# Seven half-block products for eight in the second mixture of an attention-and-two-mixtures kernel

## The chip, the cores and the metric

The kernel runs on one core of a Trainium2 chip. The metric is device time in microseconds (us), from the start of the program to its end; less is better. A core has a matrix engine (TensorE, PE in the profile; its weight loads are PEld), a vector engine (VectorE, DVE), an activation engine (ScalarE, ACT), GpSimd (POOL) and a queue that starts transfers (SyncE, SP). Products are collected in eight banks of PSUM, which DVE and ACT empty.

## The reference, cut to what matters

```
x  = attention(q, k, v)               # 4 batches, 8 heads, 576 positions, 64 wide -> 2304 tokens x 512
a, b = x @ w1, x @ w2                 # first mixture: 512 -> 1024
y  = ((a * b) @ w3) @ w_out           # 2304 x 512
h  = max(y @ v1, y @ v2, y @ v3)      # second mixture: 512 -> 768
out = h @ v_out                       # 768 -> 512
```

All data are float32 on both sides, and the weights reach the chip as 64-bit words from which the kernel makes 32-bit numbers.

## The kernel before, in words

The kernel has two halves. Attention and the first mixture are woven together, then comes the second mixture ("B" in the code), which is what the change rewrites.

Tokens lie along the free axis, in chunks of N = 512 columns (four of 512, one of 256). A number is kept as two parts, a high part that the matrix engine takes whole and the rest (`split`, L351: the high part on ACT at L352, the low part on DVE at L354). One product of a 128x128 weight block with a chunk is therefore three matmuls (`mm3`, L358 to L361).

For each chunk and each f of the hidden width, `front` (L648) makes the products with w1 and w2 (first mixture) or v1, v2, v3 (second), 12 matmuls each. The first product is copied out of PSUM by ACT (L663), the others are multiplied in, or joined by maximum, by DVE (L665). The result is split into g. `back` (L670) multiplies g by the output weights into four banks that stay open over all f; it runs one f behind. `finish_a` (L692) writes y to DRAM, `load_y` (L725) reads it back in the order of the output, and `finish_b` (L713) copies the last result out and stores it.

Weights of the second mixture are made at the end of the first: `pair` (L385) loads two 512 KB blocks of words into the place of weights that are no longer used, turns them into float32 (`float32`, L372: one ACT and four DVE instructions), and splits them. They then stay in SBUF for all chunks.

The order of all instructions is worked out ahead by a planner (`Program`, L111): each task has an engine and an estimated cost, PE tasks marked `chained` keep the order of the program, everything else is placed by how late it may be. `order` (L150) tries 30 plans, the later ones with random shifts, and keeps the one with the earliest modelled end. So any change of the tasks draws a new plan for the whole kernel, attention included. A tile that reuses a slot waits for the slot's last tile to be finished. All transfers but those of L410 are issued by SP, in order.

Of the kernel before, what the change touches and what calls it, by code (L numbers as in the profile page):

```python
# [61 lines left out]
N = 512  # L62
# [7 lines left out]
LAG = 1  # L70
MM = 0.175
# [13 lines left out]

class Tile:


    def __init__(self, slot, shape, dtype, name, ap=None):
        self.among = slot if isinstance(slot, list) else None  # L90
        self.slot = None if self.among else slot
        self.shape, self.dtype, self.name, self.ap = shape, dtype, name, ap
        self.before = self.slot.last.tasks if self.slot and self.slot.last else []
        if self.slot:
            self.slot.last = self
        self.tasks, self.touched, self.left = [], [], None

    def __call__(self):
        if self.ap is None:
# [8 lines left out]
class Program:  # L108
# [8 lines left out]
    def add(self, options, fn, reads=(), writes=(), chained=False, size=0):  # L117
# [14 lines left out]
        for what, writing in ((reads, False), (writes, True)):  # L132
            for x in what:
# [6 lines left out]
                x.tasks.append(t.n)  # L140
        deps.discard(t.n)
# [8 lines left out]
    def order(self, rounds=30):  # L150
# [8 lines left out]
        best, shift, tries = None, {}, Random(0)  # L159
# [131 lines left out]
def attention_moe_kernel(ctx, tc, q0, k0, v0, mask0, ql, kl, vl, mask, qkp, vp, w12, w3t, wo, m123, mo, out):  # L291
# [19 lines left out]
    xr, gr, cvr, zr, er, orr = ring("x", 2), ring("g", 2), ring("cv", 2), ring("z", 2), ring("e", 1), ring("o", 2)  # L311
    tqr, kr, qr, vwr, vdr = ring("tq", 2), ring("k", 4), ring("q", 4), ring("vw", 2), ring("vd", 3)
# [4 lines left out]
    others = banks[4:]  # L317

# [39 lines left out]
    def mm3(o, whi, wlo, xhi, xlo, first, last):  # L358
        nc.tensor.matmul(o, wlo, xhi, start=first, stop=False)  # L359
        nc.tensor.matmul(o, whi, xlo, start=False, stop=False)  # L360
        nc.tensor.matmul(o, whi, xhi, start=False, stop=last)  # L361
# [142 lines left out]
    def slab(n):  # L504
# [64 lines left out]
        for h2 in range(HP // 2):  # L569
# [23 lines left out]
            for ch, c0, c1 in spans(n):  # L593
                c, w = n * SL + c0 - ch * N, c1 - c0
                part = lambda i, h2=h2, xt=xs["A", ch], c=c, w=w: xt()[:, i, h2 * 2:h2 * 2 + 2, c:c + w]
                split(lambda part=part: part(0), lambda part=part: part(1),
                      lambda x32=x32, c0=c0, c1=c1: x32()[:, :, c0:c1], 2 * w, [x32], xs["A", ch])
# [4 lines left out]
    def weights_product():  # L602
# [21 lines left out]
        for half in range(2):  # L624
            prog.group += 1
            os = [Tile(b, [P, 512], F32, "pw") for b in acc]
# [21 lines left out]
    def front(kind, ch, f):  # L648
        prog.group += 1
        xt, n = xs[kind, ch], WIDTHS[ch]  # L650
        ws = [wa[f, i] if kind == "A" else wb[f, i] for i in range(2 if kind == "A" else 3)]
        z, pps = zr.tile([P, N], F32, "z"), []
        for i, (dw, w) in enumerate(ws):
            pp = bank("pf")

            def products(e, w=w, pp=pp):
                for k in range(KX):
                    c = slice(k * P, (k + 1) * P)
                    mm3(pp()[:, :n], w()[:, 0, c], w()[:, 1, c], xt()[:, 0, k, :n], xt()[:, 1, k, :n], k == 0, k == KX - 1)

            prog.add(mm(n, 12), products, [dw, xt], [pp], chained=True)
            if i == 0:
                prog.add(act(n), lambda e, pp=pp: e.copy(z()[:, :n], pp()[:, :n]), [pp], [z])  # L663
            else:
                prog.add(psum(n), lambda e, pp=pp: e.tensor_tensor(  # L665
                    z()[:, :n], pp()[:, :n], z()[:, :n], op=ALU.mult if kind == "A" else ALU.max), [pp], [z])
        g = gs[kind, ch, f] = gr.tile([P, 2, N], F32R, "g")
        split(lambda: g()[:, 0, :n], lambda: g()[:, 1, :n], lambda: z()[:, :n], n, [z], g)

    def back(kind, ch, f):  # L670
        prog.group += 1
        g, n = gs[kind, ch, f], WIDTHS[ch]
        dw, w = wa[f, 2] if kind == "A" else wb[f, 3]
        last = (NF if kind == "A" else NF2) - 1
        if f == 0:
            accs[0] = [Tile(b, [P, N], F32, "py") for b in acc]
        os = accs[0]
        for l in range(KX):

            def products(e, l=l):  # L680
                c = slice(l * P, (l + 1) * P)
                mm3(os[l]()[:, :n], w()[:, 0, c], w()[:, 1, c], g()[:, 0, :n], g()[:, 1, :n], f == 0, f == last)

            prog.add(mm(n, 3), products, [dw, g], [os[l]], chained=True)
        if f == last:
            for l in range(KX):
                (finish_a if kind == "A" else finish_b)(ch, l, os[l])

    y_dram = [[Tile(None, None, F32, "y", dram.tile([P, NB2, S], F32, name=f"y_dram{r}_{l}")) for l in range(KX)]
              for r in range(NR)]  # L690

    def finish_a(ch, l, src):  # L692
        o, n = orr.tile([P, N], F32, "o"), WIDTHS[ch]
# [200 lines left out]
```

## Time and profile before

| | us |
|---|---|
| median of 3 runs | 801.55 (801.49 to 803.25) |
| the profiled execution | 803.03 |
| its span, first to last instruction | 801.0 |
| PE busy in the span | 761.4 |
| DVE busy | 373.9 |
| ACT busy | 299.9 |

The profiled execution took 2.03 us more than its span. Matmuls overlap, so the duration of one (about 0.39 us for 512 columns) is longer than the spacing at which they follow each other; spacing is what counts for a stream of them. "Granted clock" is the share of full TensorE speed that the chip allowed in a stretch (1.00 is 2.4 GHz, 0.50 is 1.2 GHz).

### The profile page before, as it was taken

Reading aid. Unit: us, or ns where it says so; the run is one execution under the profiler, and the core shown is the slowest. Engines: PE = TensorE matmul, PEld = TensorE weight load, DVE = VectorE, ACT = ScalarE, POOL = GpSimd, SP = SyncE. Lnnn points to the kernel's source line nnn. Section 1 sums busy time; section 2 is a strip of 40 time slices with the busy share of each in tenths; the row PEclk is TensorE's granted clock in tenths of the full one; section 3 lists DMA queues with packets and bytes.
Section 4 is the critical chain, followed back from the end, with each engine's and each line's share of the span. In section 5 each row is a group of like instructions: output and inputs, shape, how many; then the busy total and the mean of one; then the engine's idle time right before and its main releaser. Section 6 shows DMA issues by size and latency. Waiting matters only on the chain.

```text
span 801.0 us, 15559 instructions
## 1 busy us (share of the span) xinstructions
PE 761.4 (95%) x6512; PEld 597.7 (75%) x6512; DVE 373.9 (47%) x672; ACT 299.9 (37%) x691; POOL 52.1 (7%) x130
## 2 busy tenths in 40 slices
PE   2989769999999989999999999999999999999997
PEld 0434458777777778777888899888888888888897
DVE  5899978456322543244421469995211322211211
ACT  3475746455425542454211346542201401121021
POOL 1220320022000210010000000000000000000000
PEclk9989859999999999999999999999999999999999
DMA  9897631033311322111330098401100100010010
GB/s 342 232 364 256 168 75 51 31 94 54 95 38 49 84 55 68 51 24 29 95 102 0 4 316 312 138 1 52 60 1 0 54 1 0 1 53 0 1 53 28
DMA packets 52390, 68.78 MB, mean 86 GB/s; under 512 B 23712, under 2 KB 39072, under 8 KB 52320
## 3 DMA queue, kind: packets, MB, share of 16 engines
q1 hardware_dynamic: 47712, 64.25, 24.6%
q0 software_dynamic: 4608, 3.55, 3.2%
q8 instruction: 51, 0.84, 0.5%
q14 instruction: 19, 0.16, 0.1%
HBM read 58.33 MB, written 9.44 MB: 85 GB/s over the span
## 4 chain that ended last, share of the span: by engine, by line
PE 87%; DMA 5%; SPq 2%; ACT 2%; DVE 2%; issue 1%; POOL 0%; ACTq 0%; DVEq 0%
PE pf L359 18%; PE pf L360 17%; PE pf L361 17%; PE py L359 7%; PE py L360 7%; PE py L361 7%; PE pw L632 4%; PE poq L579 3%; SPq L331 2%; DMA raw<-w3t 2%; PE sq L537 2%; DMA vd<-vp 1%; PE po L484 1%; PE sp L435 1%; PE pp L474 1%
## 5 line engine op out<-in xcount | busy, mean ns | idle before, releaser
L665 DVE TENSOR_TENSOR z<-pf,z 128x512 f32<-128x512 f32 (+1 forms) x100 | 63.8, 638 | 301.2 <-PE pf L361 289.2
L360 PE MATMUL pf<-yt,w 128*128 128x512 f32 (+1 forms) x360 | 134.0, 372 | 0.0
L359 PE MATMUL pf<-yt,w 128*128 128x512 f32 (+1 forms) x360 | 134.0, 372 | 0.0
L361 PE MATMUL pf<-yt,w 128*128 128x512 f32 (+1 forms) x360 | 133.9, 372 | 0.0
L359 PE MATMUL pf<-xt,w 128*128 128x512 f32 (+1 forms) x320 | 122.1, 382 | 0.0
L360 PE MATMUL pf<-xt,w 128*128 128x512 f32 (+1 forms) x320 | 120.1, 375 | 0.0
L361 PE MATMUL pf<-xt,w 128*128 128x512 f32 (+1 forms) x320 | 120.0, 375 | 0.0
L352 ACT CAST g<-z 128x512 fp32r<-128x512 f32 (+1 forms) x70 | 40.5, 578 | 157.1 <-DVE z L665 156.9
L663 ACT COPY z<-pf 128x512 f32<-128x512 f32 (+1 forms) x70 | 38.1, 544 | 155.9 <-PE pf L361 155.5
L632 PE MATMUL pw<-wf 128*128 128x512 f32 x128 | 61.3, 635 | 17.6 <-DVE wf L382 17.6
L359 PEld LDWEIGHTS pf<-yt,w 128*128 128x128 f32 x360 | 67.7, 188 | 13.1
L360 PEld LDWEIGHTS pf<-yt,w 128*128 128x128 f32 x360 | 67.8, 188 | 13.0
L361 PEld LDWEIGHTS pf<-yt,w 128*128 128x128 f32 x360 | 67.7, 188 | 13.0
L359 PEld LDWEIGHTS pf<-xt,w 128*128 128x128 f32 x320 | 61.1, 191 | 13.0 <-issue 1.0
L361 PEld LDWEIGHTS pf<-xt,w 128*128 128x128 f32 x320 | 60.9, 190 | 11.9
L360 PEld LDWEIGHTS pf<-xt,w 128*128 128x128 f32 x320 | 61.1, 191 | 11.3
L359 PE MATMUL py<-g,wp 128*128 128x512 f32 (+1 forms) x160 | 63.4, 396 | 1.2 <-ACT o L694 1.2
L354 DVE TENSOR_TENSOR g<-z,g 128x512 fp32r<-128x512 f32 (+1 forms) x70 | 44.5, 635 | 36.0 <-ACT g L352 36.0
L632 PEld LDWEIGHTS pw<-wf 128*128 128x128 f32 x128 | 25.3, 204 | 47.8 <-issue 28.4
L360 PE MATMUL py<-g,wp 128*128 128x512 f32 (+1 forms) x160 | 59.7, 373 | 0.0
L361 PE MATMUL py<-g,wp 128*128 128x512 f32 (+1 forms) x160 | 59.6, 372 | 0.0
L410 POOL DMA_DIRECT2D vd<-vp x48 | 41.0, 907 | 125.7 <-DMA vd<-vp 92.0
(80 smaller groups left out, 1005.8 us busy)
## 6 DMA issues: line engine op xcount, KB each, us to landing
qk<-qkp SPq DMA_DIRECT2D x16, 576.0 KB, 4.3
raw<-m SPq DMA_DIRECT2D x18, 512.0 KB, 5.7
raw<-w3t SPq DMA_DIRECT2D x16, 512.0 KB, 10.3
raw<-w SPq DMA_DIRECT2D x16, 512.0 KB, 4.4
y<-y_dram SPq DMA_DIRECT2D x16, 288.0 KB, 4.3
raw<-wo SPq DMA_DIRECT2D x8, 512.0 KB, 8.1
vw<-vl SPq DMA_DIRECT2D x128, 30.0 KB, 2.3
vd<-vp POOLq DMA_DIRECT2D x48, 72.0 KB, 3.0
```

What stands on the lines that cost most here:

```text
L331: prog.add([("SP", 0.36)], lambda e: e.dma_start(dst(), src()), reads, writes, size=size)
L352: prog.add(act(n), lambda e: e.copy(hi(), src()), reads, [(writes, ("hi", id(hi)))])
L354: psum(n) if from_psum else either(n), lambda e: e.tensor_tensor(lo(), src(), hi().bitcast(F32), op=ALU.subtract),
L359: nc.tensor.matmul(o, wlo, xhi, start=first, stop=False)
L360: nc.tensor.matmul(o, whi, xlo, start=False, stop=False)
L361: nc.tensor.matmul(o, whi, xhi, start=False, stop=last)
L410: lambda e, r=r: e.dma_start(vd().rearrange("p h n -> p (h n)"), vp[rd, i, r // 2, :, r % 2 * 2 * P:(r % 2 + 1) * 2 * P], **({"accum_op": ...
L537: e.matmul(sps[a]()[j * 32:(j + 1) * 32, (half * HP + hp) * BK:(half * HP + hp + 1) * BK], q[h, t:t + 32], k[h, t:t + BK], start=True, sto ...
L579: e.matmul(pos[u]()[a * D:(a + 1) * D, i * BQ:(i + 1) * BQ], vw()[h, a, i], pt().rearrange("p a n -> p (a n)")[h, c:c + BQ], start=True, s ...
L632: e.matmul(os[i](), w()[:, i * P:(i + 1) * P], o(), start=n == 0, stop=n == NF - 1)
L663: prog.add(act(n), lambda e, pp=pp: e.copy(z()[:, :n], pp()[:, :n]), [pp], [z])
L665: prog.add(psum(n), lambda e, pp=pp: e.tensor_tensor(z()[:, :n], pp()[:, :n], z()[:, :n], op=ALU.mult if kind == "A" else ALU.max), [pp], [z])
```

## The change

N becomes 504, so that there are four chunks of 504 and one of 288. In the second mixture the four large chunks are taken as two pairs (G = 0: chunks 0 and 1, G = 1: chunks 2 and 3). For each pair, each weight w of the three and each p of three, the product (f = p and f = p + 3) x (512 inputs) x (two chunks) is a 2x2 by 2x2 product of blocks, which is done with seven block products of six matmuls each and additions on DVE (Winograd's form). The 288-column chunk keeps the plain products (`rest_front`).

- `sums_of_x` reads y from DRAM and keeps seven split blocks for each pair: four of y itself or its sums named B11, B22, B21, T1 to T4.
- `convert` turns weights into float32, makes the four sums S1 to S4, splits all eight blocks and writes them to DRAM as ready parts. Five of nine (p, w) units are converted before the second mixture (EARLY), the other four and v_out in its course.
- `fetch` reads a unit's ready weights back, 1 MB for A11 to A22 (two places, in turn) and 1 MB for S1 to S4 (one place).
- h is stored to DRAM by (p, G) when the maximum over the three is done, and `final` reads it back, splits it and makes the last product after all fronts, chunk order 0, 1, 4, 2, 3.
- The planner tries 60 plans with another random seed, and several buffers share areas (`Part`).

```diff
-N = 512
+N = 504
+EARLY = 5
-    def order(self, rounds=30):
+    def order(self, rounds=60):
-        best, shift, tries = None, {}, Random(0)
+        best, shift, tries = None, {}, Random(1)
...
+    def convert(srcs, sums, hl, to):
+        raw = words(vws[0], srcs, "raw")
+        cv = cvr.tile([P, 1024], F32, "cv")
+        float32(raw, cv, cv)
+        at = lambda t, i: t()[:, i * 256:(i + 1) * 256]
+        two = [(cv, to[0])]
+        if sums:
+            sm = cvr.tile([P, 1024], F32, "cv")
+            for o, x, y, op in ((0, (cv, 2), (cv, 3), ALU.add), (1, (sm, 0), (cv, 0), ALU.subtract),
+                                (2, (cv, 0), (cv, 2), ALU.subtract), (3, (cv, 1), (sm, 1), ALU.subtract)):
+                prog.add(dve(256), lambda e, o=o, x=x, y=y, op=op: e.tensor_tensor(at(sm, o), at(*x), at(*y), op=op),
+                         [x[0], y[0]], [sm])
+            two.append((sm, to[1]))
+        for src, d in two:
+            for h in range(2):
+                w = hl.tile([P, 2, 2, 256], F32R, "hl")
+                split(lambda w=w: w()[:, :, 0], lambda w=w: w()[:, :, 1],
+                      lambda src=src, h=h: src()[:, h * 512:(h + 1) * 512].rearrange("p (b n) -> p b n", b=2), 512, [src], w)
+                dma(lambda d=d, h=h: d()[:, h * 1024:(h + 1) * 1024],
+                    lambda w=w: w().rearrange("p b h n -> p (b h n)").bitcast(F32), [w], [(d, h)], P * 4096)
...
+    def products_of(unit, x, names, pp, first):
+        i, name = names
+        w = unit[i // 4]
+        tiles, at = x[name]
+        def products(e):
+            for k in range(2):
+                c = slice(k * P, (k + 1) * P)
+                mm3(pp()[:, :N], w()[:, i % 4, 0, c], w()[:, i % 4, 1, c], at(0, k), at(1, k), first and k == 0, k == 1, not first)
+        prog.add(mm(N, 6), products, [w, *tiles], [pp], chained=True)
...
+    def halves_front(unit, w, x, zs, temps, G, p):
+        t1, u2, t5, u3 = (temps.tile([P, N], F32, "t") for _ in range(4))
+        b1, b2, b3, b4 = (Tile(everywhere, [P, 512], F32, "pb") for _ in range(4))
...
+        def second():
+            product((A12, "B21"), b1, False)
+            if w == 0:
+                copy(z11, b1)
+            else:
+                add(z11, z11, b1, ALU.max)
+        if G:
+            product((S2, "T2"), b2, True)
+        product((A11, "B11"), b1, True)
+        copy(t1, b1)
+        if not G:
+            product((A22, "T4"), b4, True)
+            second()
+            product((S2, "T2"), b2, True)
+        add(u2, t1, b2)
+        product((S1, "T1"), b3, True)
+        copy(t5, b3)
+        product((S3, "T3"), b2, False)
+        add(u3, t1, b2)
+        product((S4, "B22"), b3, False)
+        if G:
+            product((A22, "T4"), b4, True)
+            second()
+        for z, to, c, d in ((z21, t1, u3, b4), (z12, u2, u2, b3), (z22, u3, u3, t5)):
+            if w == 0:
+                add(z, c, d)
+            else:
+                add(to, c, d)
+                add(z, z, to, ALU.max)
...
+    for u, (p, w) in enumerate(b_units):
...
+        for G in range(2):
+            halves_front(units[u], w, xg[G], zs[G], temps, G, p)
+        rest_front(units[u], w, zs[2], p)
+        if done < len(b_units):
+            converted(done)
+            done += 1
+        elif done < len(b_units) + HF:
+            i = done - len(b_units)
+            convert([mo[2 * i], mo[2 * i + 1]], False, hl, [m_dram[i]])
+            done += 1
+        fetch_a(u + 2)
+        fetch_s(u + 1)
...
+    for i, ch in enumerate((0, 1, 4, 2, 3)):
+        final(ch, g_places[i % 3], stage_g, ms)
```

In the diff `copy` is an ACT copy out of PSUM and `add` is a DVE instruction on 504 columns.

## Rows read from the trace of the kernel before

**Rows 1.** The page: busy time of PE; the chain that ended last, by engine.
```profile
PE 761.4 (95%) x6512; PEld 597.7 (75%) x6512; DVE 373.9 (47%) x672; ACT 299.9 (37%) x691; POOL 52.1 (7%) x130
...
PE 87%; DMA 5%; SPq 2%; ACT 2%; DVE 2%; issue 1%; POOL 0%; ACTq 0%; DVEq 0%
```

**Rows 2.** Windows: stretch, length, busy per engine, granted clock, DMA share, GB/s.
```profile
100.00:120.00 20.00, 13.53 (x414) 11.62 (x409) 14.71 (x33) 9.92 (x15) 4.75 (x17) 0.50 0.37 75
...
456.00:492.00 36.00, 35.17 (x287) 34.12 (x287) 27.93 (x53) 18.50 (x39) 0.00 (x0) 1.00 0.84 295
...
548.00:604.00 56.00, 56.00 (x242) 45.14 (x241) 14.43 (x34) 11.96 (x34) 0.00 (x0) 1.00 0.12 41
```

**Rows 3.** Timeline, second mixture: start, duration, engine, line; 48 matmuls between each two.
```profile
521.73 0.39 PE L359 MATMUL py<-g,w 128*128 128x512 f32 x1
...
532.93 0.40 PE L359 MATMUL py<-g,w 128*128 128x512 f32 x1
...
776.38 0.28 PE L359 MATMUL py<-g,w 128*128 128x256 f32 x1
...
782.00 0.28 PE L359 MATMUL py<-g,w 128*128 128x256 f32 x1
```

**Rows 4.** The tile yt's first and last product; then the timeline's last matmul.
```profile
L359 PE MATMUL pf<-yt,w x360: 276/393/404, 492.4 to 792.9; 128*128 128x512 f32 x144, 128*128 128x256 f32 x36
...
796.03 0.28 PE L361 MATMUL py<-g,w 128*128 128x256 f32 x1
```

**Rows 5.** Groups of instructions by shape: busy us, mean ns of one, idle before.
```profile
L665 DVE TENSOR_TENSOR z<-pf,z 128x512 f32<-128x512 f32 x80 | 55.3, 691 | 270.2 <-PE pf L361 258.2 <-ACT z L663 6.4 <-PE pp L474 5.6
L354 DVE TENSOR_TENSOR w<-cv,w 128x512 fp32r<-128x512 f32 x40 | 26.5, 684 | 2.2 <-ACT w L352 2.1
L665 DVE TENSOR_TENSOR z<-pf,z 128x256 f32<-128x256 f32 x20 | 8.5, 423 | 31.0 <-PE pf L361 31.0
L382 DVE SCALAR_TENSOR_TENSOR cv<-raw,cv 128x1024 uint32<-128x1024 uint32 x20 | 24.5, 1223 | 0.3
L377 DVE TENSOR_SCALAR cv<-cv 128x1024 f32<-128x1024 f32 x20 | 13.7, 685 | 1.5 <-ACT cv L376 1.4
L663 ACT COPY z<-pf 128x512 f32<-128x512 f32 x56 | 32.9, 587 | 136.3 <-PE pf L361 135.9
```

**Rows 6.** Timeline: a product's last matmul and its copy; ACT then DVE; ACT then PE.
```profile
560.68 0.39 PE L361 MATMUL pf<-yt,w 128*128 128x512 f32 x1
...
561.17 0.59 ACT L663 COPY z<-pf 128x512 f32<-128x512 f32 x1 [0.89 <-PE pf L361]
...
568.64 0.63 ACT L352 CAST g<-z 128x512 fp32r<-128x512 f32 x1
...
569.31 0.69 DVE L354 TENSOR_TENSOR g<-z,g 128x512 fp32r<-128x512 f32 x1 [1.91 <-ACT g L352]
...
465.46 0.58 ACT L694 COPY o<-py 128x512 f32<-128x512 f32 x1
...
466.09 0.39 PE L359 MATMUL py<-g,wp 128*128 128x256 f32 x1 [0.68 <-ACT o L694]
```

**Rows 7.** DMA issues, KB each, median us to landing; then raw's landing times.
```profile
qk<-qkp SPq DMA_DIRECT2D x16, 576.0 KB, 4.3
raw<-m SPq DMA_DIRECT2D x18, 512.0 KB, 5.7
...
DMA to landing us min/median/max: 4.3/6.3/12.0
```

**Rows 8.** Tile x, the attention result: its DVE additions, first and last start.
```profile
L588 DVE TENSOR_TENSOR x<-poq,od x48: 344/348/359, 98.0 to 455.1; 128x192 f32<-128x192 f32 x48
```

**Rows 9.** Waits of PE, longest: for whom, total, times, longest one.
```profile
PE pw L632 <- DVE wf L382: 17.6, 2, 15.9
PE poq L579 <- issue: 4.6, 3, 2.4
```

More of the change, by code (lines that the diff above doesn't have):

```diff
@@ L722, in attention_moe_kernel @@
[L722 to L742 removed]
+                o = orr.tile([P, N], F32, "o")
@@ L781, in attention_moe_kernel, with converted @@
+    b_units = [(p, w) for p in range(HF) for w in range(3)]
+    hl = Ring(tqr.slots)
+    early = EARLY
+    def converted(u):
+        p, w = b_units[u]
+        convert([m123[w, p], m123[w, p + HF]], True, hl, w_dram[u])
+    for n in range(len(a_units) + LAG):
+        if n < len(a_units):
+            ch, f = u = a_units[n]
+            if f == 0:
+                x_of(ch + 1)
             front(*u)
         if n >= LAG:
-            back(*units[n - LAG])
-        while gone and gone[0][0] <= n:
-            _, p, f, i = gone.pop(0)
-            wb[f, i], wb[f, i + 1] = pair(place[p], [m123[j, f] if j < 3 else mo[f] for j in (i, i + 1)])
+            back(*a_units[n - LAG])
@@ new lines, in attention_moe_kernel @@
+    for u in range(early):
+        converted(u)
+    xp = xr.slots
+    stage = [xp[2], xp[3]] if NW % 2 else [xp[0], xp[1]]
+    last = [xp[0], xp[1]] if NW % 2 else [xp[2], xp[3]]
+    a_places, s_place = [place[1], place[4]], place[10]
+    z_slots = [er.slots[0], dpr.slots[0], sr.slots[0], ptr.slots[0]]
+    temps = Ring(zr.slots + orr.slots + loose)
+    g_parts = [p for s in gr.slots for p in parts(s, 2, N)]
+    z_sets = [z_slots, g_parts]
+    z_rest = odr.slots[0]
+    units = {u: [None, None] for u in range(len(b_units))}
@@ new lines, in fetch_a, with fetch_s @@
+    def fetch_a(u):
+        if u < len(b_units):
+            units[u][0] = fetch(a_places[u % 2], w_dram[u][0], "wu")
+    def fetch_s(u):
+        if u < len(b_units):
+            units[u][1] = fetch(s_place, w_dram[u][1], "wu")
+    fetch_a(0)
+    fetch_s(0)
+    xg = [sums_of_x(0, kq, iter([place[i] for i in (6, 7, 8, 2, 3, 9, 0)]))]
+    fetch_a(1)
+    xg.append(sums_of_x(1, stage, iter([*kq, place[5], place[11], *last, stage[0]]), [(y, NW - 2) for y in y_dram]))
+    prog.group += 1
+    n = WIDTHS[-1]
@@ new lines, in attention_moe_kernel @@
+    done = early
+    for u, (p, w) in enumerate(b_units):
+        if w == 0:
+            zs = [[Tile(s, [P, N], F32, "zb") for s in z_sets[G]] for G in range(2)]
+            zs.append(Tile(z_rest, [P, 2, n], F32, "zb"))
+        for G in range(2):
[10 more added lines that the diff above has]
+        fetch_s(u + 1)
@@ L787, in attention_moe_kernel @@
+    ms = [fetch(p, d, "wm") for p, d in zip([a_places[len(b_units) % 2], s_place, stage[1]], m_dram)]
+    out_places = [p for s in (*last, *kq, place[11]) for p in parts(s, 5, T)]
+    stage_g = Ring(parts(vws[0], 4, N))
+    g_places = [[place[i] for i in p] for p in ((6, 7, 8), (2, 3, 9), (0, 5, 1))]
+    for i, ch in enumerate((0, 1, 4, 2, 3)):
+        final(ch, g_places[i % 3], stage_g, ms)
     order = prog.order()
```

274 lines of the change are left out of this document (185 added, 89 removed).

## The prediction, on record before the changed kernel ran

> **What bounds the kernel now.** I read the busy times and the chain that ended last first: PE is busy 761 of 801 us and holds 87% of the chain, while DVE and ACT are under half [rows 1]. An average hides stages, so the windows come next: around 110 us PE waits and runs at half clock, at the handover to the second mixture it loses under 1 us, and in the second mixture it is busy without a gap at full clock while DVE works a quarter of the time [rows 2]. So the part that the change rewrites is a pure stream of matmuls, and its length is their number times their spacing. The timeline gives the spacing: 48 matmuls of 512 columns take 532.93 - 521.73 = 11.20 us, 0.2333 each; 48 of 256 take 5.62 us, 0.117 each [rows 3]. Spacing goes with columns, with no fixed part to speak of. As a test: 1440 matmuls (1152 wide, 288 narrow) make 268.8 + 33.7 = 302.5 us, and the trace has 796.15 - 492.4 = 303.7 from the first to the end of the last spacing [rows 4].
>
> **Products.** By the same slope 504 columns take 0.2297 us and 288 take 0.1315. The first mixture's matmuls cover the same 2304 columns, so it stays: 288 x (4 x 0.2333 + 0.117) = 302.5 before, 288 x (4 x 0.2297 + 0.1315) = 302.5 after. In the second, 18 (p, w, G) groups have 7 x 6 = 42 matmuls of 504 for 48: 756 x 0.2297 = 173.6. The remainder has 216 x 0.1315 = 28.4, the last product 288 x 0.2297 + 72 x 0.1315 = 75.6. Sum 277.7, a gain of 24.8 us. This is all that the change can give.
>
> The row shows 0.2333 us for 512 columns at clock 1.00 [rows 2, 3]. The Trainium skill, "TensorE: Matmul & The Clock Gate", section "Back-to-back issue gap", has columns / 2.4 GHz plus 2.5 ns, 0.2125 for 504; by that the 108 matmuls saved would be worth 22.95, and the sum 1.9 us worse. The trace disagrees with the rule's 0.2158 for 512, and I keep the trace's.
>
> **DVE's new work.** Before, DVE's part in the second mixture was a side job. Now a (p, w) unit has 2 x 42 matmuls of 504 and 24 of 288, 19.3 + 3.15 = 22.45 us of PE. DVE has per G, for w of 1 and 2, two sums u2 and u3, one maximum and three pairs of sum and maximum, 9 instructions of about 0.69 (128x512 out of PSUM, 0.691), 6.2 us; for w = 0 five, 3.4. The remainder adds two of 0.42 to 0.46 [rows 5]. A conversion costs DVE 2 x 0.685 + 2 x 1.223 + 4 x 0.423 + 4 x 0.684 = 8.25 [rows 5]. So units 1 and 2, with a conversion each, load DVE with 12.4 + 0.9 + 8.25 = 21.5 of 22.45 us; units 0 and 3 with 15, the later ones with 12 to 18.4 (a conversion of the output weights, without sums, is 5.2). In all about 148 of 202 us: DVE doesn't bound, but it is no longer idle when PE needs it.
>
> **The wait that the form brings.** S3 x T3 is added onto the bank that holds S2 x T2, so it waits until DVE has read that bank for u2; u2 itself needs t1, ACT's copy of A11 x B11. In G = 1 the order is S2T2, A11B11, S1T1, S3T3. Count from the start s of the last matmul of A11B11. The copy starts at s + 0.49 (561.17 after 560.68) and takes 0.587; DVE follows within 0.04 and takes 0.691; the next matmul can start 0.05 after, and has lost its early weight load, 0.11 more (0.39 for 0.28) [rows 5, 6]. That is s + 1.97. S1T1 covers up to s + 7 x 0.2297 = s + 1.61. So PE stands 0.36 us in each of nine G = 1 groups, 3.2 us, even with DVE free. What is late next is u3, which nothing waits for within the group. In G = 0 A11B11 comes three products earlier: u2 starts right after S2T2, done at s + 0.49 + 0.69, free at s + 1.34 of 1.61; 0.27 of slack. The b3 bank has one ACT copy in between, the same slack or more.
>
> **DVE's queue ahead of it.** An instruction of DVE can't be broken off. In G = 1 u2 falls into the tail of G = 0 (six instructions for w of 1 and 2): half of 0.69, 0.35, on each of six groups, 2.1; elsewhere a conversion's instruction (up to 1.22) may lie ahead in some 4 of 10 cases: about 0.2 over twelve groups, 2.4, less what the slack of G = 0 takes: 1.2. I take 3.3, bounds 0 (everything falls into gaps) and 18 x 1.22 = 22.
>
> **Reading weights back.** The A weights have two places and a unit's 22 us to arrive: nothing, unless SP is held; then the S weights below are late first. The S weights have one place: `fetch_s` can start when G = 1 has finished S4 x B22, and the next unit wants S2 after A22T4, A12B21, the remainder and three products: 5 x 1.38 + 3.15 = 10.05 us. On SP it stands behind conversions' stores, which wait for ACT and DVE. No row has 1 MB; 576 KB land in 4.3 us, 512 KB in a crowd in 5.7 [rows 7]. So 1 MB takes 4.3 (all latency) to 11.4 (two of the crowded ones); I take the first row scaled, 7.6, since a unit moves some 5 MB in 22 us, 240 GB/s, less than the 295 of the handover [rows 2]. That fits; for the share that meets a conversion's loads I put 1.5 us over nine units, bounds 0 and 9 x (11.4 + 0.4 - 10.05) = 16. The Trainium skill, "DMA: Bandwidth & Descriptors", section "Measured (HBM→SBUF, 128 partitions, SWDGE, issued from GpSimd)", gives 6.15 us for 1 MB; by it this term is nothing and the sum 1.5 us better. No run here shows 1 MB yet.
>
> **The handover.** Five conversions (41 us of DVE), four 504x2 additions and seven splits for each pair (about 1.22 each by the slope of the rows, 27 us), the last chunk's own work (7) and unit 0's (8) make 83 us. They must be done by the first remainder, 38 us of last chunk plus 19 of unit 0, 57 us after the fourth chunk ends. They fit only if conversions start in the fourth chunk, and these use the buffers of the last attention slab. In the trace before, that slab ended at 455, just in time [rows 8]; nothing forced it to, and a planner that sees its late times can bring it forward. I take 1.5 us, bounds 0 and 83 - 57 = 26. At the other end, h of the last unit goes to DRAM and back under G = 1 and the remainder, 12.8 us, against two transfers of about 4 and a split: 0.5 us. The last copies and stores are as long as before.
>
> **The new plan.** Attention's order is drawn anew. PE's waits before 120 us are the largest there, 15.9 the longest [rows 9]. They come from loads and conversions that the change doesn't touch, so I take 0 with 5 either way.
>
> **Sum.** 803.03 - 24.8 + 3.2 + 3.3 + 1.5 + 1.5 + 0.5 = 788.2 for the profiled execution; this lay 1.48 above its median, so 786.7: I say 787. Its own range, from the small ends and the redraw, is 779 to 794.
>
> **Rivals.**
> (a) DVE's order bounds the converting units. For: 21.5 of 22.45 us leaves no room. Against: a unit is needed only five units later, so the planner may spread conversions. If each of the seven units with a conversion grows 1.5 us more, 797.
> (b) Slower: the S fetch, one place, waits in SP's and the transfers' queues behind a conversion's 3 MB. It decides from a landing of about 12 us on, where nine waits of 2 us take the gain; raw's longest, half the size, was 12.0 [rows 7]. At 13 us each unit waits 3: 787 + 27 - 1.5 = 812.
> (c) The last slab stays late, and 83 us of DVE meet 57: 787 + 26 - 1.5 = 811. Against: DVE is nearly free in the fourth chunk.
> (d) It doesn't do what it says: 504 columns cost as much as 512, for instance since their rows start off a boundary. Then 2160 matmuls of both mixtures lose 0.0036 each: 795.
> (e) PE stands only for the 3.2 us of the form, and the new plan is better by 4: 776.
> (f) The short stops lower the clock. The rows: at 100 to 120 us PE stood a third of the time and the clock was at 0.50; at 456 to 492 it lost 0.8 us and kept 1.00 [rows 2]. One unit at half clock costs 22 us: 809. The Trainium skill, "TensorE: Matmul & The Clock Gate", section "Loop structure matters more than you think", wants dense products and counts evacuation by DVE as harmless; but here a product waits for the evacuation, which speaks against the change.
>
> **How the numbers follow.** Forecast 0.55; (a) 0.15; (b) 0.08; (c) 0.05; (d) 0.05; (e) 0.10; (f) 0.02. A measurement of this kernel can tell about 0.3%, 2.4 us, from no change. (b), (c), (f) are slower: 0.15. Of (a) a third reaches 799 and more: same 0.06. The rest is faster, 0.79. The range leaves out the far ends of (e) below 777 and of (b), (c) and (f) above 805.
>
> **What would show it.** Right: 756 matmuls of 504 at 0.230 us; first to last product of the second mixture 285 to 290 us; nine waits of PE for DVE's u2 of about 0.4 us and more where conversions run. (b) would show as PE waiting for the weights' DMA ahead of S2 with the landing over 10 us; (c) as a wait of PE at the first remainder or G = 1; (d) as 0.233 at 504; (f) as a granted clock below 1.00 after 500 us. What would prove me wrong altogether: waits in the stage before 490 us that the old plan didn't have, over 5 us.

## The result and the profile after

| | before | after |
|---|---|---|
| median, us | 801.52 (800.25 to 803.25) | 791.43 (786.67 to 791.95) |
| profiled execution | 803.03 | 790.95 |
| its span | 801.0 | 788.9 |
| PE busy | 761.4 | 742.7 |
| DVE busy | 373.9 | 479.9 |

The ratio is 0.986, with a 95% interval of 0.9817 to 0.9902. The change is faster by 10.1 us in the medians and by 12.1 us in the two profiled spans. The forecast was 787, a gain of 14.8 us in the span.

The page of the changed kernel (busy time; the chain that ended last; the read of ready weights: issues, KB, median us to landing):

```profile
PE 742.7 (94%) x6404; PEld 587.0 (74%) x6404; DVE 479.9 (61%) x834; ACT 321.5 (41%) x701; POOL 52.5 (7%) x130
...
PE 78%; DVE 10%; DMA 5%; issue 4%; ACT 2%; SPq 1%; POOL 0%; POOLq 0%; DVEq 0%; ACTq 0%
...
wu<-w_dram SPq DMA_DIRECT2D x18, 1024.0 KB, 5.2
```

Against [rows 1], PE has 108 matmuls fewer and 18.7 us less work, DVE 106 us more, and DVE's part of the chain has gone from 2% to 10%: PE now waits for it in places. The same stretches as in [rows 2], with the same columns, of the changed kernel:

```profile
100.00:120.00 20.00, 13.65 (x464) 11.87 (x462) 16.11 (x34) 13.50 (x26) 4.77 (x17) 0.53 0.66 175
456.00:492.00 36.00, 35.26 (x250) 34.07 (x249) 31.49 (x44) 22.19 (x36) 0.00 (x0) 1.00 0.73 252
548.00:604.00 56.00, 54.77 (x258) 45.33 (x257) 43.65 (x69) 16.66 (x27) 0.00 (x0) 1.00 0.86 298
```

In the third line PE, which was busy for all of the 56 us, has lost 1.2, DVE has gone from 14 to 44 us and the transfers from 41 to 298 GB/s. The clock stays at 1.00, its level of 2.4 GHz.

Then the stages. Three tile rows of the changed kernel (line, tile, count: shortest/median/longest ns, first and last start): first mixture, products of the second, last product.

```profile
L390 PE MATMUL pf<-xt,w x320: 291/391/788, 121.6 to 496.9; 128*128 128x504 f32 x128, 128*128 128x288 f32 x32
...
L390 PE MATMUL pb<-xc,wu x324: 288/390/502, 501.1 to 707.7; 128*128 128x504 f32 x126, 128*128 128x288 f32 x36
...
L390 PE MATMUL pb<-gg,wm x120: 290/390/397, 708.1 to 782.7; 128*128 128x504 f32 x96, 128*128 128x288 f32 x24
```

The second mixture begins at 501.1. Before, its first matmul was at 492.4 [rows 4], but twelve matmuls of the first mixture (1.4 us at 0.117) came after that one, so the comparable point is 493.8. That gives an account of the two spans ("spacing" is the number of matmuls times their distance; before, PE had no stop in the second mixture):

| | before | after | difference | forecast |
|---|---|---|---|---|
| first mixture ends at | 493.8 | 501.1 | **+7.3** | 0 |
| second mixture, matmuls by spacing | 302.35 | 276.5 | -25.85 | -24.8 |
| stops of PE among its products | 0 | 5.8 | +5.8 | +6.5 |
| S fetch, handover, last product | - | 0 | 0 | +3.5 |
| from the last matmuls' end to the end | 4.85 | 5.5 | +0.65 | 0 |
| sum | 801.0 | 788.9 | -12.1 | -14.8 |

The stretch that the change was about did better than forecast. What is missing was lost before it begins, in a stage whose products the change does not rewrite.

PE's waits in the changed kernel (line, for whom, total, times, longest):

```profile
PE pw L664 <- DVE wf L413: 20.4, 3, 16.0
...
PE pw L664 <- DVE wp L385: 4.0, 2, 3.3
PE pb L390 <- DVE t L829: 2.6, 7, 0.8
```

`pw` is the product of the two weight matrices w3 and w_out that the kernel makes in its first 100 us, in two halves on the same four banks of PSUM. It waited 17.6 us before [rows 9] and now 24.4, 6.8 more. Its last matmul starts at 96.1, for 89.3 before: 6.8 later too. The wait for `wp`, the split that empties the banks of the first half, was not there before at all. (Line 664 is the product, 385 and 413 belong to splits and conversions, 829 to DVE's sums in the halves.)

### The profile page after: what moved, and what is told of

It reads as the page before. It is cut to its first block, busy times and chain, and to the rows that moved or that the text cites. A ratio compares the mean times of both kernels' runs of the same rounds, so it can differ in the third digit from the quotient of the medians.

```text
span 788.9 us, 15758 instructions
## 1 busy us (share of the span) xinstructions
PE 742.7 (94%) x6404; PEld 587.0 (74%) x6404; DVE 479.9 (61%) x834; ACT 321.5 (41%) x701; POOL 52.5 (7%) x130
## 4 chain that ended last, share of the span: by engine, by line
PE 78%; DVE 10%; DMA 5%; issue 4%; ACT 2%; SPq 1%; POOL 0%; POOLq 0%; DVEq 0%; ACTq 0%
PE pb L390 10%; PE pb L391 10%; PE pb L392 10%; PE pf L390 9%; PE pf L391 8%; PE pf L392 8%; PE py L390 4%; PE py L391 4%; PE py L392 4%; PE poq L610 3%; PE pw L664 2%; DVE t L829 2%; DMA vd<-vp 2%; PE sq L568 2%; DMA raw<-w3t 1%
## 5 line engine op out<-in xcount | busy, mean ns | idle before, releaser
L390 PE MATMUL pf<-xt,w 128*128 128x504 f32 (+1 forms) x320 | 123.7, 386 | 0.0
L390 PE MATMUL pb<-xc,wu 128*128 128x504 f32 (+1 forms) x324 | 120.7, 373 | 2.8 <-DVE t L829 2.6
L391 PE MATMUL pf<-xt,w 128*128 128x504 f32 (+1 forms) x320 | 121.5, 380 | 0.2 <-DVE xt L385 0.2
L392 PE MATMUL pf<-xt,w 128*128 128x504 f32 (+1 forms) x320 | 121.3, 379 | 0.0
L391 PE MATMUL pb<-xc,wu 128*128 128x504 f32 (+1 forms) x324 | 119.7, 369 | 0.0
L392 PE MATMUL pb<-xc,wu 128*128 128x504 f32 (+1 forms) x324 | 119.5, 369 | 0.0
L697 DVE TENSOR_TENSOR z<-pf,z 128x504 f32<-128x504 f32 (+1 forms) x40 | 25.5, 637 | 105.3 <-PE pf L392 98.3
L390 PEld LDWEIGHTS pb<-xc,wu 128*128 128x128 f32 x324 | 60.8, 188 | 17.5 <-DVE t L829 7.7
L390 PEld LDWEIGHTS pf<-xt,w 128*128 128x128 f32 x320 | 61.8, 193 | 12.3 <-issue 1.4
L391 PEld LDWEIGHTS pf<-xt,w 128*128 128x128 f32 x320 | 61.7, 193 | 10.8 <-DVE xt L385 0.7
L392 PEld LDWEIGHTS pf<-xt,w 128*128 128x128 f32 x320 | 61.6, 193 | 10.9
L392 PEld LDWEIGHTS pb<-xc,wu 128*128 128x128 f32 x324 | 60.9, 188 | 10.1
L391 PEld LDWEIGHTS pb<-xc,wu 128*128 128x128 f32 x324 | 60.9, 188 | 9.6
L390 PE MATMUL py<-g,wp 128*128 128x504 f32 (+1 forms) x160 | 62.7, 392 | 0.7 <-ACT o L718 0.7
L831 ACT COPY t<-pb 128x504 f32<-128x504 f32 x36 | 20.9, 581 | 96.0 <-PE pb L392 94.9
L391 PE MATMUL py<-g,wp 128*128 128x504 f32 (+1 forms) x160 | 59.4, 372 | 0.3 <-DVE g L385 0.3
L392 PE MATMUL py<-g,wp 128*128 128x504 f32 (+1 forms) x160 | 59.3, 371 | 0.0
L829 DVE TENSOR_TENSOR t<-t,pb 128x504 f32<-128x504 f32 x60 | 40.6, 676 | 29.7 <-PE pb L392 25.6
L695 ACT COPY z<-pf 128x504 f32<-128x504 f32 (+1 forms) x40 | 21.7, 542 | 70.8 <-PE pf L392 70.8
L383 ACT CAST g<-z 128x504 fp32r<-128x504 f32 (+1 forms) x40 | 23.1, 577 | 53.6 <-DVE z L697 53.3
```

The costliest lines, as they stand in the source:

```text
L383: prog.add(act(n), lambda e: e.copy(hi(), src()), reads, [(writes, ("hi", id(hi)))])
L390: nc.tensor.matmul(o, wlo, xhi, start=first, stop=False, skip_group_check=again)
L391: nc.tensor.matmul(o, whi, xlo, start=False, stop=False, skip_group_check=again)
L392: nc.tensor.matmul(o, whi, xhi, start=False, stop=last, skip_group_check=again)
L697: prog.add(psum(n), lambda e, pp=pp: e.tensor_tensor(z()[:, :n], pp()[:, :n], z()[:, :n], op=ALU.mult), [pp], [z])
L829: prog.add(dve(N), lambda e: e.tensor_tensor(ap(o), ap(x), ap(y), op=op), [x, y], [o])
```

## The experiments

All medians below are from runs beside the kernel before on the same chip; the interval is that of the ratio. "Ends at" is the end of the first mixture as in the table, "fronts" the time from there to the last product.

| kernel | median, us | ratio to before (95%) | ends at | fronts | pw's last matmul |
|---|---|---|---|---|---|
| before | 801.5 | 1 | 493.8 | - | 89.3 |
| after | 791.43 | 0.986 (0.9817 to 0.9902) | 501.1 | 207.0 | 96.1 |
| r1: before, other seed | 801.86 | 0.9994 (0.9972 to 1.0015) | 492.6 | - | 90.0 |
| l1: before, shared areas | 802.35 | 1.0011 (0.9998 to 1.0025) | 491.6 | - | 88.9 |
| b3: before, banks free | 810.89 | 1.012 (1.0084 to 1.0155) | 504.8 | - | 99.0 |
| r2: after, seed 0 | 791.89 | 0.9861 (0.9799 to 0.9923) | 499.9 | 209.6 | 99.9 |
| r3: after, seed 2 | 788.66 | 0.9827 (0.9782 to 0.9872) | 500.0 | 205.6 | 96.8 |
| w1: after, order of two products | 788.69 | 0.9818 (0.9763 to 0.9874) | 504.7 | 201.9 | 99.1 |
| d1: after, EARLY = 3 | 793.68 | 0.9902 (0.9874 to 0.9929) | 503.3 | 208.4 | 99.6 |
| d1: after, EARLY = 7 | 793.97 | 0.9906 (0.9878 to 0.9933) | 499.5 | 210.8 | 96.8 |
| p1: after, eighth product | 807.94 | 1.0088 (1.0054 to 1.0121) | 495.5 | 225.8 | 96.8 |
| f1: after, S fetched twice | 827.42, one run | - | 500.3 | 243.9 | 96.7 |
| b1: after, banks held | 787.77 | 0.9835 (0.9804 to 0.9866) | 489.5 | 212.3 | 89.7 |
| b2: b1 + w1, seed 7 | 787.27 | 0.9821 (0.9795 to 0.9847) | 497.7 | 206.3 | 91.9 |

### Is the late first mixture the luck of one plan?

The change also doubles the planner's tries and changes its seed. First the old kernel with the new seed and tries:

```diff
-    def order(self, rounds=30):
+    def order(self, rounds=60):
...
-        best, shift, tries = None, {}, Random(0)
+        best, shift, tries = None, {}, Random(1)
```

> The kernel before, with the planner's new seed and 60 tries and nothing else. Its first mixture ended at 493.8 us of its span, that of the changed kernel at 501.1, 7.3 us later, which is half of what the products gained. Theory R (a new draw of the plan moves the stage up to there by several us either way, whatever else is changed): this end moves by 3 us or more, and the whole time with it, since the second mixture stays at 302 us; 795 to 808. Rival L (the shared buffers, 504 columns and the earlier last slab cost the 7 us, a draw next to nothing): the end stays within 492 to 496 and the time within 0.3% of 801.5.

Measured: 801.86 us, and the first mixture ends at 492.6. The seed alone moves nothing that can be measured. Then the new kernel with two other seeds, 0 and 2 for 1:

```diff
-        best, shift, tries = None, {}, Random(1)
+        best, shift, tries = None, {}, Random(0)
```

> The changed kernel with the planner's old seed (60 tries), nothing else. Theory R: the first mixture ends 3 us or more away from 501.1, between 491 and 507, and the time follows; the second mixture, fronts and last product, stays at 282 us within 2. Rival L: the end stays at 499 to 503 and the time at 791 within 2.

> The changed kernel with another seed (2), nothing else. As for the old seed: theory R wants an end of the first mixture 3 us or more away from 501.1 in at least one of the two, rival L wants both at 499 to 503. The second mixture stays at 282 us within 2 by both.

r3 is the same edit with Random(2). Measured: 791.89 and 788.66, with the first mixture ending at 499.9 and 500.0. Each of three seeds has it 6 to 7 us late, and pw's last matmul at 96 to 100. A single bad draw is out; something in the tasks themselves makes all three draws late.

### Is it the sharing of areas, or the conversions made early?

The change puts several buffers into shared areas. The old kernel with those areas, and its old sizes and tasks:

```diff
+class Part(Slot):
...
+    kq, loose = slots(sb, "kq", 2), slots(sb, "lo", 2)
+    areas = [Tile(s, [P, 2008], F32, "area") for s in kq]
+    kqs = [Part(a, i * KEYS) for a in areas for i in range(3)] + loose
+    vws = slots(sb, "vw", 1)
+    tqr, kr, qr, vwr = ring("tq", 2), Ring(kqs[::2]), Ring(kqs[1::2]), Ring(parts(vws[0], 2, 1024))
...
-    tqr, kr, qr, vwr, vdr = ring("tq", 2), ring("k", 4), ring("q", 4), ring("vw", 2), ring("vd", 3)
```

> The kernel before with the changed kernel's shared buffers for k, q, values and raw words alone (several tiles as parts of one area), plan and all else as before. Theory B (parts of one area wait for each other more than tiles of their own, and this is where the first mixture lost 7.3 us): the first mixture ends at 498 to 502 us for 493.8, the time is 806 to 809. Rival E (early conversions pull attention ahead): the end stays at 492 to 495 and the time within 0.3% of before.

Measured: 802.35, ratio 1.0011, first mixture at 491.6, 2.2 us earlier than in the profiled execution of before. The order of its instructions is that of before, so 2 us is also the measure of what two executions of one order differ by. The profiled executions differ by the same 2.2 us, 803.03 and 800.85: in this pair all of the difference lies ahead of the second mixture. Sharing is out.

Five conversions, 41 us of DVE by the forecast, now stand ahead of the second mixture. If they press the first, three should end it earlier and seven later:

```diff
-EARLY = 5
+EARLY = 3
```

> The changed kernel with three units converted before the second mixture for five, six in it for four. Theory E (the planner brings attention forward so that the last slab's buffers are free for conversions, and pays in the head and in a lower clock): with less to convert the first mixture ends earlier, 495 to 499 us for 501.1, and the last slab is later than 416. The fronts lose more, since two more units carry a conversion: 6.5 to 9 us for 5.8. Theory B: the end stays at 499 to 502, only the fronts change.

> The changed kernel with seven units converted before the second mixture for five, two in it for four. Theory E: the first mixture ends later, 502 to 506 us, or PE waits at the handover for the two more conversions, 16.5 us of DVE. The fronts lose less, 3.5 to 5 us, since only the waits of the form and those of five units are left. Theory B: the end stays at 499 to 502.

Measured: it ends at 503.3 with three and at 499.5 with seven, the opposite sign, by 2.2 and 1.6 us, about what two executions of one order differ by. This theory fell too. Both kernels lose at the handover: their fronts are 1.4 and 3.8 us longer than the changed kernel's. With three, PE waits 2.8 us there for ACT's copy `t`; with seven, 3.5 us.

### Two lines that choose banks

What was left in the full diff were two lines that neither the prediction nor the core of the diff shown above has:

```diff
-            os = [Tile(b, [P, 512], F32, "pw") for b in acc]
+            os = [Tile(acc, [P, 512], F32, "pw") for _ in acc]
...
-            accs[0] = [Tile(b, [P, N], F32, "py") for b in acc]
+            accs[0] = [Tile(acc, [P, N], F32, "py") for _ in acc]
```

A tile made on a given bank `b` knows which tile had it last, and the planner's graph gets an edge from that one's tasks. A tile made on "one of `acc`" gets its bank only when the plan is laid, so the edge from the first half of pw to the second, and from there to the first result of the first mixture, is not in the graph. The planner then does not see that the splits of the first half hold up the second half. The test is to put only these two lines into the old kernel (b3), and to put only the edges back into the new one (b1):

```diff
+    held = []
+
+    def taken(tiles):
+        now = list(tiles)
+        for t, last in zip(now, held):
+            t.before = last.tasks
+        held[:] = now
+        return now
...
-            os = [Tile(acc, [P, 512], F32, "pw") for _ in acc]
+            os = taken(Tile(acc, [P, 512], F32, "pw") for _ in acc)
...
-            accs[0] = [Tile(acc, [P, N], F32, "py") for _ in acc]
+            accs[0] = taken(Tile(acc, [P, N], F32, "py") for _ in acc)
```

> The kernel before with one thing of the changed kernel: the four banks of the weights product and of the running result are chosen by the planner among four instead of being given one by one, so that its graph has no edge from the weights product's first half to its second and to the first running result; old seed, 30 tries. Its plan then has the weights product end at 98.5 us for 93.1, as all plans of the changed kernel have it. Theory G (these missing edges let attention go ahead of the weights product and cost the first mixture its 7 us): the first mixture ends at 497 to 501 us for 493.8, the time is 805 to 809. Rival (the second half's new tasks or the 504 columns draw the plan so): the end stays at 491 to 495, the time within 0.3%.

> The changed kernel with these edges put back in its graph (banks still chosen by the planner), all else as it was. Its plan has the weights product end at 92.9 us. Theory G: the first mixture ends at 495 to 498 us for 501.1, and the time is 786 to 788, if the fronts keep their 207. Rival: the end stays at 499 to 503.

Measured: the old kernel with the two lines is slower by 1.2% and ends its first mixture at 504.8, 11.0 us later. The new kernel with the edges back ends it at 489.5, 11.6 us earlier than the change. The stretches from 50 to 100 and from 100 to 130 us with PE alone (busy, matmuls done, granted clock, DMA share, GB/s), first of before, then of b3:

```profile
50.00:100.00 50.00, 45.87 (x533) 0.94 0.75 240
100.00:130.00 30.00, 23.53 (x452) 0.63 0.37 84
```

```profile
50.00:100.00 50.00, 44.38 (x390) 0.90 0.58 193
100.00:130.00 30.00, 21.45 (x551) 0.55 0.56 151
```

and of the change, then of b1:

```profile
50.00:100.00 50.00, 44.87 (x430) 0.97 0.62 204
100.00:130.00 30.00, 23.40 (x540) 0.54 0.54 140
```

```profile
50.00:100.00 50.00, 47.29 (x540) 0.94 0.74 246
100.00:130.00 30.00, 25.70 (x455) 0.63 0.40 100
```

All five kernels with the edges did 486 to 630 matmuls in the first 50 us (before, r1, l1, b1, b2), all nine without 390 to 430; before and l1, of one order, differ by 97 there. The clearer sign is pw's last matmul, at 88.9 to 91.9 with the edges and at 96.1 to 99.9 without. The wait says where the time went; b3's waits of PE:

```profile
PE pw L632 <- DVE wf L382: 20.6, 3, 16.2
PE pw L632 <- DVE wp L354: 4.8, 2, 2.5
```

The wait for `wp` is there in each of the nine, 3.7 to 5.7 us; before, r1 and b1 have none of it, l1 0.5, b2 2.5. The wait for `wf` is no sign: it is as long in b1 (20.9) as in b3. So the cause is shown both ways, with one plan each: the two lines added alone to the old kernel, and their edges alone put back into the new one. That it acts through the splits that come late is what the waits say. It is not all of it: in the second stretch the half clock of 1.2 GHz lasts longer without the edges, 0.55 and 0.54 granted for 0.63. Up to 490 us PE was busy 455.1 us before, 452.1 in the change, 449.1 in b3 and 458.7 in b1. So of the change's 7.3 us some 3 are idle time and, by an estimate from the clock, 30 x 0.09 = 2.7 the clock. Attention's order shifts with the edges too, and how much the wait for `wp` and how much the shift brings was not separated. Each of the two lines by itself was not tried.

The 11 us are more than median executions would show. b3's profiled execution was the slowest of its four, 3.0 us above its median, and b1's the fastest, 2.9 below. If such differences lie ahead of the second mixture, as between before and l1, the first mixtures of median executions end at about 492.3 (before), 501.8 (b3), 501.6 (the change) and 492.4 (b1): an estimate of 9 us both ways. The same step explains p1, which has no edges and ends at 495.5, earlier than b2 with them at 497.7: p1's profiled execution was 3.6 us below its median, so it belongs at about 499.

### Where b1's gain went

b1 gained 11.6 us before the second mixture, some 9 by the estimate for median executions, and is only 3.7 us below the change in the median, with overlapping intervals. Its fronts take 212.3 for 207.0, which is the rest. Its timeline at the handover (start, duration, engine and line; in brackets idle time before and who ended it):

```profile
496.82 0.50 PE L390 MATMUL pb<-xc,wu 128*128 128x504 f32 x1 [0.30 <-DVE t L838]
...
498.07 0.39 PE L392 MATMUL pb<-xc,wu 128*128 128x504 f32 x1
...
499.73 0.62 ACT L383 CAST hl<-cv 128x512 fp32r<-128x512 f32 x1 [3.20 <-DMA w_dram<-hl]
...
502.22 1.03 ACT L383 CAST xc<-area 128x1008 fp32r<-128x1008 f32 x1 [1.88 <-DVE area L801]
...
503.16 0.57 ACT L840 COPY t<-pb 128x504 f32<-128x504 f32 x1
...
503.79 0.79 PE L390 MATMUL pb<-xc,wu 128*128 128x504 f32 x1 [5.32 <-ACT t L840]
504.37 0.62 PE L391 MATMUL pb<-xc,wu 128*128 128x504 f32 x1
```

At 498.07 PE ends S3 x T3 and wants the bank that ACT's copy of S1 x T1 empties. S1 x T1 was done before 496.82, where S3 x T3 begins; the copy starts at 503.16. On ACT's queue a conversion's split stands ahead, which waits 3.20 us for its buffer `hl` to be stored, and then a split of x, which waits 1.88 us for DVE's sum. After the stop the matmuls take 0.79 and 0.62 for 0.39, and the next ten follow each other at 0.58 to 0.42 us for 0.23, 2 us lost in all. A window over it shows the granted clock, third number from the end:

```profile
496.00:510.00 14.00, 8.38 (x28) 6.13 (x27) 11.73 (x18) 4.84 (x8) 0.00 (x0) 0.76 0.70 244
```

The same wait, for ACT's `t`, is 3.0 us in r2, 2.8 and 3.5 in the two with EARLY of 3 and 7, and 2.3 in b2. It is the prediction's rival (c) in small: work that must be ready at the handover is late. That an earlier end of the first mixture brings it out is what b1 suggests; it is not shown as a rule, since the kernel with EARLY of 3 ends at 503.3 and waits, and p1 ends at 495.5 and does not.

### The stop that the form brings

S3 x T3 goes onto the bank of S2 x T2 and waits for DVE's u2, which needs ACT's copy of A11 x B11. w1 puts A11 x B11 one product earlier in G = 1:

```diff
-        if G:
-            product((S2, "T2"), b2, True)
         product((A11, "B11"), b1, True)
         copy(t1, b1)
+        if G:
+            product((S2, "T2"), b2, True)
```

> The changed kernel with A11 x B11 ahead of S2 x T2 in G = 1 too, so that ACT's copy runs under a product. Theory (the wait for u2 is ACT's copy and DVE's sum in one product's cover): the nine waits of PE in G = 1, 0.28 to 0.7 us each and most of the 5.8 us that the fronts lose, go; the fronts take 202 to 203.5 us for 207.0. Rival (they are DVE busy with other work): waits of the same number and 4 to 6 us in all remain. The whole time follows by 4 us, but for the new draw of the plan before 500 us.

The change has eleven stops in its fronts, 5.8 us in all: one in each of the nine G = 1 groups, two in G = 0. One in its smallest form, G = 1 of a later unit, from the changed kernel's timeline, and then one of G = 0 where a conversion is in the way:

```profile
606.17 0.39 PE L392 MATMUL pb<-xc,wu 128*128 128x504 f32 x1
...
606.60 0.58 ACT L831 COPY t<-pb 128x504 f32<-128x504 f32 x1 [4.89 <-PE pb L392]
...
607.21 0.68 DVE L829 TENSOR_TENSOR t<-t,pb 128x504 f32<-128x504 f32 x1
...
607.53 0.40 PE L392 MATMUL pb<-xc,wu 128*128 128x504 f32 x1
...
607.95 0.50 PE L390 MATMUL pb<-xc,wu 128*128 128x504 f32 x1
608.28 0.39 PE L391 MATMUL pb<-xc,wu 128*128 128x504 f32 x1
...
552.57 0.39 PE L392 MATMUL pb<-xc,wu 128*128 128x504 f32 x1
...
553.25 1.22 DVE L413 SCALAR_TENSOR_TENSOR cv<-raw,cv 128x1024 uint32<-128x1024 uint32 x1
...
553.94 0.38 PE L392 MATMUL pb<-xc,wu 128*128 128x504 f32 x1
...
554.39 0.67 DVE L829 TENSOR_TENSOR t<-t,pb 128x504 f32<-128x504 f32 x1
...
555.12 0.49 PE L390 MATMUL pb<-xc,wu 128*128 128x504 f32 x1 [0.79 <-DVE t L829]
```

At 607.53 to 607.95 the spacing is 0.42 for 0.23, and the next is 0.33: 0.19 of wait and 0.10 for the weight load that could not run ahead, 0.29 us (it starts at 607.94, with its matmul; the loads before it start 0.22 ahead). In the second, S2 x T2 is finished with the matmul at 552.57, but a conversion's instruction of 1.22 us starts at 553.25 and u2 only at 554.39; PE, done with S1 x T1 at 553.94, loses 0.95 + 0.10.

w1's fronts take 201.9 us for 207.0, and the sum of the spacings is 201.2. Its waits of PE for DVE's `t` are down from 2.6 us in 7 to

```profile
PE pb L390 <- DVE t L829: 0.2, 1, 0.2
```

So the stop is shown to be the form's order of products, and one product of lead removes it. In this kernel the first mixture ended at 504.7, 3.6 later than in the change, so the median of 788.69 does not show all of the 5 us.

### What the saved products are worth

p1 makes an eighth product of six matmuls in each group (A11 x B11 once more, onto a bank that is open, which changes the result):

```diff
             product((A22, "T4"), b4, True)
+            product((A11, "B11"), b1, False)
             second()
...
         copy(t5, b3)
+        if G:
+            product((A11, "B11"), b1, False)
         product((S3, "T3"), b2, False)
```

> The changed kernel with an eighth block product in each of the 18 groups: A11 x B11 again onto its own bank, in G = 1 right ahead of S3 x T3 (the result is changed by that). By the spacing of the changed kernel the fronts get 18 x 6 x 0.2283 = 24.7 us of matmuls more, and lose the waits of G = 1, since u2 gets the cover of two products: 226 to 228 us for 207.0, the time about 809 with 4 either way for the plan. That would say that the change without its saved products is some 7 us slower than the kernel before. If the products saved are worth 22.95 (columns by 2.4 GHz and 2.5 ns each), the fronts take 224 to 225.5.

Its tile row:

```profile
L390 PE MATMUL pb<-xc,wu x360: 292/388/398, 495.5 to 720.9; 128*128 128x504 f32 x144, 128*128 128x288 f32 x36
```

The longest matmul is 398 ns, where a matmul after a stop takes up to 502 in the change, and PE has no wait for `t` in its list: there is no stop, since the added product covers it. The fronts take 225.8 us; 201.2 plus 108 x 0.2283 = 24.7 is 225.9. So a product costs what its spacing says, and the whole change without the saved ones is slower than the kernel before, 807.94 us, ratio 1.0088 (1.0054 to 1.0121).

### The room of the S fetch

f1 fetches the S weights of each unit but the first twice into the one place:

```diff
-            units[u][1] = fetch(s_place, w_dram[u][1], "wu")
+            w = units[u][1] = fetch(s_place, w_dram[u][1], "wu")
+            if u:
+                dma(lambda: w().rearrange("p b h n -> p (b h n)").bitcast(F32), lambda: w_dram[u][1](), [w_dram[u][1]], [w], P * 8192)
```

> The changed kernel with each fetch of S weights but the first made twice into its place, one after the other, 2 MB for 1 MB. The fetch of 1 MB lands in 5.2 us and has 10 us of cover, so PE never waited for it. Theory (a landing of 10 us is where it decides): two take 10.5 to 11 us with the second one's start, so PE waits 0.5 to 2 us ahead of S2 in eight units, 4 to 16 us in all, and the time is 795 to 807. Rival (other transfers set the landing and there is much more room): no wait, 789 to 793.

Measured: 827.42 us in one run, 20 more than the upper end expected, and PE waits for the weights, which it never does in the change. One unit of its timeline (SP's issues of 1 MB each, then PE's first matmul on S2) and its row of waits:

```profile
611.45 0.33 SPq L362 DMA_DIRECT2D wu<-w_dram  x1
...
617.37 0.32 SPq L362 DMA_DIRECT2D wu<-w_dram  x1
...
621.18 0.38 SPq L362 DMA_DIRECT2D wu<-w_dram  x1
...
629.26 0.76 PE L390 MATMUL pb<-xc,wu 128*128 128x504 f32 x1 [7.80 <-DMA wu<-w_dram]
```

```profile
PE pb L390 <- DMA wu<-w_dram: 28.6, 5, 8.4
```

Two landings of 5.7, the median here, would be 11.4 us, little over the 10.05 of room. By the order of the program the first issue is the S fetch, the second the next A fetch and the third the S fetch again, into the same place, which waits for the first to land. That took 8.0 us; the third went out 1.7 us later, 9.7 after the first, and PE starts 8.1 after it. So here the two landings took some 8 us each and not 5.7 (the second by PE's start), with the A fetch between them, and 1.7 went by on SP's queue. Of the 37 us by which the fronts are longer 28.6 are these waits; part of the rest is a clock of 0.87 over 536 to 632 us. A single fetch has room, and rival (b)'s mechanism is real when landings grow and one waits for another.

### Both mends together

b2 has b1's edges and w1's order, with seed 7 (edits as above).

> Both mends together: A11 x B11 first in both pairs, and the edges back; seed 7, the plan of the earliest end among twelve by its own account. By theory G and the theory of the wait: first mixture to 496 us, fronts 202 us, last product 75 us, tail 5.5: a span of 779, 781 us in the runs, 20 less than the kernel before. By the rival of G: 785.

Measured: 787.27 us (785.9 to 788.17), ratio 0.9821 (0.9795 to 0.9847), 6 us above the 781 expected. It is the lowest median of all, 4.2 us below the change; but its interval and the change's overlap, so it is not shown to be the faster of the two. The first mixture ends at 497.7, the handover costs a wait of 2.3 us for ACT's `t` and some matmuls at a lower clock after it, and the fronts take 206.3.

## Why the prediction was right, and where it was not

Direction and range held (779 to 794 for the forecast itself, 777 to 805 with the rivals), and so did the mechanism in the second mixture; the gain was smaller, 10.1 of 14.5 us in the medians and 12.1 of 14.8 in the profiled spans. By its own steps:

**Products.** Right. The timeline of the changed kernel, 42 matmuls of 504 apart:

```profile
524.37 0.39 PE L390 MATMUL pb<-xc,wu 128*128 128x504 f32 x1
...
533.96 0.39 PE L390 MATMUL pb<-xc,wu 128*128 128x504 f32 x1
```

9.59 / 42 = 0.2283 us, for 0.2297 forecast by the slope. From 521.19 to 524.37, 24 matmuls of 288 columns give 0.1325 for 0.1315. So rival (d) is out: 504 columns cost less than 512, in proportion. (Its 2160 matmuls should be 1152 + 1044 = 2196, which leaves 795 as it is.) The rule of the Trainium skill, "TensorE: Matmul & The Clock Gate", section "Back-to-back issue gap", would make it 0.2125; the trace does not agree, and p1's fronts, 24.6 us longer than the sum of the spacings for 24.7 by the row's price, confirm the row. The section has the rule for a matmul by itself and about 0.131 us for 512 columns in a stream of weight loads and matmuls; with 0.2333 the trace does not agree with that either.

**The form's wait, and DVE's queue ahead.** Right in place and sum: 5.8 us for 6.5, at all nine G = 1 groups and two others. The form alone was 0.29 for 0.36 each, since the copy starts 0.43 after the last matmul's start, for 0.49; nine make 2.6. The rest, 3.2 us, is put down to DVE's queue, where 3.3 was said; DVE was busy 153.9 us of the fronts, for 148 said. w1 and p1 show that the stops are this wait.

**S fetch.** The 1.5 us were not needed: 1 MB landed in 5.2 us in the median and 8.2 at most, under the 10.05 of room, and PE never waits for it. The 6.15 us of the Trainium skill, "DMA: Bandwidth & Descriptors", section "Measured (HBM→SBUF, 128 partitions, SWDGE, issued from GpSimd)", lie nearer than the prediction's 7.6 (there the time that the transfer engines were busy, here issue to landing). Rival (b), which decides from 12 us on, did not come up.

**Handover, and fronts to last product.** Nothing was lost for the 2.0 us put there, as the stages of the change join. Rival (c)'s ground was right: DVE was free enough, and the last attention slab's last addition came forward from 455.1 [rows 8] to 416.3. But b1, b2, r2 and the EARLY kernels wait 2.3 to 5.3 us there for ACT's copy, which the prediction did not look at. From its first product to its last the second mixture took 282.3 us (207.0 + 75.3), less than the 285 to 290 given as a sign of being right.

**The new plan.** This is the step that failed: "They come from loads and conversions that the change doesn't touch, so I take 0 with 5 either way." It measured +7.3, outside the bound, and about +9.3 between median executions by the estimate above. Its reason was wrong too: the change does touch this stage, through two lines of the diff that choose banks and so take edges out of the planner's graph. The prediction's sign for "wrong altogether", waits of over 5 us before 490 that the old plan did not have, came close: the new wait, for the splits, is 4.0 us. The other 2.8 of pw's 6.8 are no sign, since r1, with the old plan's edges, waits 20.9 us for `wf` as well. The sign was also too strong, since the mechanism in the second mixture held all the same. That the total still came near is in part luck: 3.5 us of cushions (S fetch, handover, last product) were not used, and the products and stops were 1.75 better than said (1.05 and 0.7), none of which has to do with the plan.

**Clock.** Rival (f) is out for the change: 1.00 in the second mixture. Rival (a) as well: it has 10.5 us more of stops, 17 in all, and there are 5.8. (A third of its 0.15 is 0.05; the prediction counts 0.06 as "same".)

## What to carry to other kernels

Where a planner lays the order, a line that only changes how a buffer is chosen is a change of the dependency graph: read the whole diff for such lines, and compare first the stage that the change does not rewrite. When partial products are added onto a bank that another engine must read first, put the product whose copy it needs two products ahead instead of one; it adds no matmul and took the stop away here. A profiled execution is one of several: before a stage's end is compared between two kernels, see where each execution lies among the runs of its kernel. And b1's 9 to 12 us ahead of a border shrank to 3.7 in the median, with a copy late in ACT's queue behind it, so look at the queues at a border before pricing a gain ahead of it.

## What the hardware showed that was not expected

After the stop of 5.3 us in b1, matmuls of 504 columns that else take 0.39 us took 0.79 and 0.62, with a granted clock of 0.76 over 496 to 510 us, a mean between its two levels of 1.2 and 2.4 GHz. The same half clock followed the handover's stops of 2.3 us in b2, 3.0 in r2 and 3.5 with EARLY of 7; the stop of 2.8 with EARLY of 3 and the 0.3 to 1.1 us stops of the change left the clock at 1.00. So a stop can cost more than itself, and its length alone does not say whether it will; what decides was not tested. A read of 1 MB from DRAM landed in 5.2 us in the median while the core moved 298 GB/s in all (548 to 604 us), less than by scaling the 576 KB of [rows 7]. And one order of instructions, that of before and of l1, ended its first mixture at 493.8 and 491.6 in two executions; such 2 us are not explained here.
